# Attention of block 0 first, sixteen plain weight chunks for blocks 0 and 1, and block 1's projection with two tiles in flight

## The chip, the cores and the metric

The kernel runs on one core of one Trainium2 chip. The metric is the device time of one execution in microseconds (us). The engines are PE (TensorE, matrix products into PSUM banks), DVE (VectorE), ACT (ScalarE), POOL (GpSimd) and SP (SyncE, which here only issues transfers). Each engine works through its own queue in order: an instruction that waits holds up all that stand behind it.

## The reference

One pre-LN block in float32, for one sequence of 2048 tokens of width 576, with 32 heads of width 18:

```python
def _A_ref(x, wqkv, wo):
    ...
    W, dil = 8, 2
    idx = pos[:, None] - off[None, :]          # off = arange(W) * dil
    logits = jnp.einsum("bhsd,bhswd->bhsw", q, kg) * scale
    logits = jnp.where(mask[None, None, :, :], logits, -1e9)
    attn = _softmax(logits, axis=-1)
    o = jnp.einsum("bhsw,bhswd->bhsd", attn, vg)
    return (lambda x, *d: x.transpose(*d))(o, 0, 2, 1, 3).reshape(B, S, D) @ wo

def _B_ref(x, w_gate, w_up, w_down):
    g = jnp.einsum("bsd,df->bsf", x, w_gate)
    u = jnp.einsum("bsd,df->bsf", x, w_up)
    h = _sigmoid(g) * u
    return jnp.einsum("bsf,fd->bsd", h, w_down)

h = x + _A_ref(_layernorm(x, axis=-1), A_wqkv, A_wo)
h2 = h + _B_ref(_layernorm(h, axis=-1), B_w_gate, B_w_up, B_w_down)
```

A token sees itself and seven tokens before it, two apart. The hidden width F of the gated part is 4608.

## The kernel before

**Tiling.** Since the window steps by two, even and odd tokens never meet. The tokens fall into four blocks of 512: blocks 0 and 1 are the two halves of the even tokens, blocks 2 and 3 those of the odd ones. A block is four tiles of 128 tokens. Every product in full precision is built of three fast ones: an operand is split into a high part (ACT, L100) and the rest (DVE, L101), by the function `split`; the tiles `th` and `tl` hold split activations, `qw`, `w` and `d` split weights.

**First part.** `ln1` normalises a block (DVE statistics, POOL's power, ACT applying them for blocks 1 to 3: L126 to L128), transposes it on PE and splits it. `qkv` computes q, k and v for one of four groups of eight heads; ACT evicts them (L346) and writes them to DRAM (`q`, `k`, `v`). `attention` reads q and windows of k and v back (`kw`, `vw`) and works on DVE alone but for one exponential on ACT: sixteen steps for one block and group. The result of block 0 stays in SBUF, the others go through `oscr`. `att_all` sets the order (0,0), (1,0), (0,1), (1,1), (0,2), (0,3), (1,2), (1,3), each (block, group); its steps are handed out between the tiles of `qkv`. The loop at the end of this part drains what is left of `att_all` and then runs block 0's output projection, `proj_j`, for four tiles at once: transpose of the attention result, split, two products with halves of `wo` (L146 to L149), residual, a second normalisation, transpose. That gives block 0's operands `a00` and `a01`.

**Second part.** The hidden width is walked in 36 chunks of 128, for two blocks at a time. A *plain* chunk (`single`, "std") handles one block: 28 products of 128x512 (tiles b) for gate and up, and 24 of 128x288 for the down product (tile `dp`). A *pair* chunk (`pair`) handles two blocks with seven products in place of eight, built from sums and differences of the two blocks' operands (`sums`, `s1` to `s4`): 50 of 128x512 and 48 of 128x288. The order of the list `items` is: NSTD plain chunks for block 0, the pair chunks NSTD to 35 for blocks 0 and 1, NSTD plain chunks for block 1, 36 pair chunks for blocks 2 and 3; NSTD is 8, so there are 80. Weights come one chunk ahead: `load_gu` loads the gate and up columns (tile `wg`, 640 KB, two buffers, issued two chunks ahead), `weights` loads the down rows (tile `wd`, 288 KB, one buffer) and splits both. `down_units` sums two chunks in PSUM, ACT copies them to `stage` (L612), and POOL adds them to DRAM with an accumulating transfer (`h<-stage`, L616).

**Background work.** Each chunk calls `bg_step` at seven places; each call takes one step of a generator. `under_first` runs under the plain chunks of block 0: `proj_scr` projects block 1, tile after tile (load of `oj`, `proj_j` in one PSUM bank `bgp`, write of `xj` to `xscr`), then `operands` reads blocks 0 and 1 back (`ar`), forms the sums and splits them. `finish_bg` empties it before the first pair chunk. `under_rest` does the same for blocks 2 and 3 under what follows: attention, projection, operands. A scheduler puts the instructions on each engine in an order of its own, by priorities (`tc.high_priority`) and a model of when operands are ready; the background work moves in this order against the chunks that emit it.

Of the kernel before, what the change touches and what calls it, by code (L numbers as in the profile page):

```python
# [14 lines left out]
F32 = mybir.dt.float32  # L15
# [37 lines left out]
HC = 700  # L53
NSTD = 8


@with_exitstack
def kernel(ctx, tc, x, wqkv, wo, wmlp, out):
# [96 lines left out]
    def attention(at, b, g, o):  # L155
# [66 lines left out]
    def proj_j(bank, oj, hj, wos, th, tl, xn_tile, put, order=(0, 1)):  # L222
        with tc.high_priority(HI):
            dve.tensor_copy(oj[:, D:DX], oj[:, DM:D])
        pv = tr_main(bank(), oj)
        with tc.high_priority(HI):
            split(th[:, 0:4], tl, pv)
        yield
        pv = tr_rest(bank(), oj)
        with tc.high_priority(HI):  # L230
            split_rest(th[:, 4], pv)
        yield
        for i in order:
            ps = bank()
            tok_major(ps, DH2, th, tl, slice(0, P), wos[i][:, 0], wos[i][:, 1])
# [12 lines left out]
        pv = tr_rest(bank(), xn)  # L248
        with tc.high_priority(HI):
            put(pv.unsqueeze(1), slice(4, 5))  # L250
        yield

    def sums(pl, ar, s1, s2, s4, rd):
        a00, a01, a10, a11 = ar[0][:, 0:2], ar[0][:, 2:4], ar[1][:, 0:2], ar[1][:, 2:4]
# [4 lines left out]
        dve.tensor_tensor(rd, ar[0][:, 4], ar[1][:, 4], ALU.subtract)  # L261
        return dict(a00=(a00, None), s2=(s2, None), s3=(a10, None), s1=(s1, None),
                    a01=(a01, ar[0][:, 4]), a11=(a11, ar[1][:, 4]), s4=(s4, rd))

# [90 lines left out]
    o = None  # L355
    emitted = set()

    def att_all():
# [8 lines left out]
    xb = load_x(0)  # L367
    w = qkv_w(0)
    T = []
    gl = ln1(0, xb)  # L370
    T.append(next(gl))
    xb = load_x(1)
    run(gl, qkv(0, 0, T[0], w))
    pads(0)
    for b in (1, 2, 3):
        if b > 1:
            xb = load_x(b)
        gl = ln1(b, xb)
        T.append(next(gl))
        drain(gl)  # L380
        if b == 1:
            drain(qkv(1, 0, T[1], w))
    ag = att_all()
    wn = qkv_w(1)
    for b in (2, 3):
        for _ in qkv(b, 0, T[b], w):
            step(ag, 2)
    pads(1)
    w = wn
    w2 = qkv_w(2)  # L390
    for b in range(4):
        for _ in qkv(b, 1, T[b], w):
            step(ag, 2)
    pads(2)
    pads(3)
    w3 = qkv_w(3)

    def wo_w(i, ww):
# [5 lines left out]
        act.dma_start(wscr[i], f32(ww))  # L404
        return ww

    wos = [None, wo_w(1, sar.tile([P, 2, 5, DH2], F32R, name="wo1"))]
    for b, g in ((0, 2), (1, 2), (0, 3), (1, 3), (2, 2), (3, 2), (2, 3), (3, 3)):
        if (b, g) == (2, 3):
            wos[0] = wo_w(0, saw.tile([P, 2, 5, DH2], F32R, tag="qw", bufs=2, name="wow"))  # L410
        for _ in qkv(b, g, T[b], w2 if g == 2 else w3):
            step(ag, 3)
    h = load_x(0)
    drain(ag)

# [5 lines left out]

    with tc.high_priority(HI):
        ar = tok_tile((P, 5, TB))
        oT = th_tile(), tl_tile()
        xn = [ev_tile([P, 2, DX]) for _ in range(2)]
        gens = []
        for j in range(NS):
            js = slice(j * P, (j + 1) * P)

            def put(pv, cs, js=js):  # L430
                act.activation(ar[:, cs, js], pv, AF.Copy)

            gens.append(proj_j(any_bank, o[:, j], h[:, j], wos, oT[0][:, :, js], oT[1][:, :, js],
                               lambda j=j: xn[j // 2][:, j % 2], put, (1, 0)))
        run(*gens)
        act.dma_start(hacc[0], h)
        act.dma_start(xscr[0], ar)
        X = {"a00": x_half(ar[:, 0:2], None), "a01": x_half(ar[:, 2:4], ar[:, 4])}
    ps_stk.close()
# [10 lines left out]
    def load_gu(f):  # L450
        ws = gw.tile([P, GU], F32, bufs=2, name="wg")
        sp.dma_start(ws, wmlp[f][:, :GU])
        return ws

    def weights(kind, f, ws):
        with tc.high_priority(HI):
            wd = gw.tile([P, D], F32, name="wd")
            sp.dma_start(wd, wmlp[f][:, GU:WC])
            r = ws.rearrange("p (c n) -> p c n", c=10)
            w1 = gw.tile([P, 2, 5, P], F32R, bufs=2, name="w1")  # L460
# [168 lines left out]

    def proj_scr(pj, blocks):  # L630
        wos = []
        for i in range(2):
            ww = pj.tile([P, 2, 5, DH2], F32R, name=f"wow{i}")
            sp.dma_start(f32(ww), wscr[i])
            wos.append(ww)

        def load(b, j):
            oj = pj.tile([P, DX], F32, bufs=2, name="oj")
            sp.dma_start(oj[:, :D], oscr[b][:, j])
            return oj  # L640

        tiles = [(b, j) for b in blocks for j in range(NS)]
        nxt = load(*tiles[0])
        for i, (b, j) in enumerate(tiles):
            e, hf = BLOCKS[b]
            oj = nxt
            hj = pj.tile([P, D], F32, name="hj")
            sp.dma_start(hj, xv[e, hf][:, j])
            if i + 1 < len(tiles):
                nxt = load(*tiles[i + 1])  # L650
            xj = pj.tile([P, 5, P], F32, name="xj")

            def put(pv, cs):
                act.activation(xj[:, cs], pv, AF.Copy)

            th = pj.tile([P, 5, P], F32R, name="oth")
            tl = pj.tile([P, 4, P], F32R, name="otl")
            yield from proj_j(lambda: gp.tile([P, 512], F32, name="bgp"), oj, hj, wos, th, tl,
                              lambda: xj.rearrange("p c n -> p (c n)"), put)
            act.dma_start(hacc[b][:, j], hj)  # L660
            act.dma_start(xscr[b][:, :, j * P:(j + 1) * P], xj)

    def operands(pp, p, Xn, names):
        ar = []
        for t in range(2):
            a = pp.tile([P, 5, TB], F32, name=f"ar{t}")
            sp.dma_start(a, xscr[2 * p + t])
            ar.append(a)
        s = [pp.tile([P, 2, TB], F32, name=f"rs{i}") for i in range(3)]
        rd = pp.tile([P, TB], F32, name="rd")  # L670
        raw = sums(pp, ar, *s, rd)
        yield
        for n in names:
# [5 lines left out]
    def under_first():  # L679
        drain_at()  # L680
        with sb_pool("pj", "right") as pj:
            yield from proj_scr(pj, (1,))
        with sb_pool("pp", "right") as pp:
            yield from operands(pp, 0, X, ("s2", "s3", "s1", "a11", "s4"))

    def drain_at():
        at_stk.close()

    Xn = {}

    def under_rest(last_x):
        with sb_pool("at2", "right") as at2:
# [4 lines left out]
            yield from ga  # L697
        with sb_pool("pj2", "right") as pj:
            yield from proj_scr(pj, (2, 3))
        pp = ctx.enter_context(sb_pool("pp2", "right"))  # L700
# [6 lines left out]
    def bg_step(i):  # L707
        nonlocal raw, phase
        if phase is ATT and i == 3:
            return  # L710
# [35 lines left out]
    wg = load_gu(1)  # L746
    seg = []
    for c, (kind, p, f) in enumerate(items):
        w, d = wc
        if c == NSTD:  # L750
            finish_bg()
            last_x = splits[-1]
            bg = under_rest(getattr(last_x, "ins", last_x))
        if c == NF:
            with tc.high_priority(HI):
                a10 = gw.tile([P, 2, TB], F32, tag="tw", name="tw")
                sp.dma_start(a10, xscr[1][:, 0:2])
                X["a10"] = x_half(a10, None)
        if c == NF + NSTD:
# [12 lines left out]
        else:  # L772
            hid = pair(X, w, units, bg_step)
            blocks = [2 * p, 2 * p + 1]
# [49 lines left out]
```

## Time and profile before

| what | value |
|---|---|
| median of three runs | 1720.25 us (1715.8 to 1725.97) |
| the execution profiled | 1719.7 us, span 1717.7 us |
| PE busy | 1611.8 us (94%) |
| DVE busy | 1145.2 us (67%) |
| ACT busy | 821.4 us (48%) |
| PE clock granted, mean | 0.97 |
| DMA | 256.64 MB, mean 149 GB/s |

The span is the time from the first to the last instruction on the chip's core; the run is some 2 us longer. The page's slices cut the span in 40 equal parts and give each engine's busy share in tenths. The chain of waits goes back from the last instruction: each row is a start, a duration and what ran or was waited for there. The first product of the second part stands at 256.3 us, the products of blocks 2 and 3 run from about 1060 us to the end.

### The profile page before, as it was taken

The page shows a single profiled execution, that of the slowest core. Times are in us where ns is not written, and L with a number is a line of the kernel's source. Part 1 is how long each engine was busy: PE and PEld are TensorE (multiplying, and loading weights), DVE is VectorE, ACT ScalarE, POOL GpSimd, SP SyncE. Part 2 cuts the span into 40 slices and gives each one's busy share as a digit, 9 for nine tenths or more (in the row PEclk, how much of TensorE's full clock was granted, in tenths as well). Part 3 has the DMA queues.
Part 4 walks back from the last instruction along what each step waited for, and adds up shares of the span by engine and source line. Part 5 has one row for each costly group of instructions (what it writes and reads, how often), then busy time and mean ns, then how long its engine had stood idle before and what let it go on. Part 6 is the DMA issues. An engine that isn't in the chain of part 4 may idle for free.

```text
span 1717.7 us, 22333 instructions
## 1 busy us (share of the span) xinstructions
PE 1611.8 (94%) x8688; PEld 1418.8 (83%) x8688; DVE 1145.2 (67%) x1769; ACT 821.4 (48%) x1419; POOL 102.9 (6%) x112
## 2 busy tenths in 40 slices
PE   5999879955999999999889989999999999999999
PEld 4999868754888888888778977888888888888888
DVE  7699889634998999998545454645454454544544
ACT  7322225422565555555335444555555555555551
POOL 2000000000000000000000000000000000000000
PEclk8999989986999999999999999999999999999999
DMA  5555545753367676665756665545645456455462
GB/s 171 201 192 207 200 151 161 232 143 121 101 162 190 155 177 161 167 156 122 224 135 156 167 185 144 139 111 118 139 101 132 111 119 137 102 127 115 115 146 83
DMA packets 86426, 256.64 MB, mean 149 GB/s; under 512 B 7857, under 2 KB 25521, under 8 KB 84529
## 3 DMA queue, kind: packets, MB, share of 16 engines
q0 software_dynamic: 19040, 82.58, 25.9%
q1 hardware_dynamic: 43856, 142.04, 25.2%
q10 hardware_dynamic: 23424, 30.61, 5.1%
q8 instruction: 68, 1.11, 0.3%
q14 instruction: 38, 0.30, 0.1%
HBM read 141.95 MB, written 115.60 MB: 150 GB/s over the span
## 4 chain that ended last, share of the span: by engine, by line
PE 67%; DVE 15%; DMA 11%; issue 3%; ACT 3%; SPq 0%; POOL 0%; ACTq 0%; DVEq 0%; POOLq 0%
PE b L488 32%; PE dp L606 22%; PE b L495 6%; DMA wd<-in_wmlp_dram 5%; PE acc L146 3%; DMA oj<-o 2%; DVE pr L168 2%; DVE lg L171 2%; PE bgp L146 2%; DVE w L101 2%; DMA wg<-in_wmlp_dram 2%; DVE pr L194 1%; DVE s L501 1%; DVE pr L199 1%; PE bgp L135 1%
## 5 line engine op out<-in xcount | busy, mean ns | idle before, releaser
L488 PE MATMUL b<-tl,w 128*128 128x512 f32 x1728 | 440.1, 399 | 24.4 <-ACT tl L100 18.6
L488 PEld LDWEIGHTS b<-tl,w 128*128 128x128 f32 x1728 | 320.9, 191 | 99.2 <-ACT tl L100 19.6
L488 PE MATMUL b<-th,w 128*128 128x512 f32 x1344 | 347.8, 393 | 5.7 <-DVE w L101 3.5
L488 PEld LDWEIGHTS b<-th,w 128*128 128x128 f32 x1344 | 248.4, 189 | 57.4 <-DVE w L101 3.9
L612 ACT ACTIVATE stage<-dp 128x576 f32<-128x576 f32 x272 | 175.0, 646 | 127.2 <-PE dp L606 121.3
L606 PE MATMUL dp<-d,h1h 128*128 128x288 f32 x1152 | 214.5, 297 | 4.2 <-ACT stage L612 2.9
L606 PE MATMUL dp<-d,h0h 128*128 128x288 f32 x1152 | 214.3, 297 | 2.2 <-ACT h0h L100 1.8
L606 PEld LDWEIGHTS dp<-d,h1h 128*128 128x128 f32 x1152 | 179.7, 190 | 11.0 <-ACT stage L612 3.4
L606 PEld LDWEIGHTS dp<-d,h0h 128*128 128x128 f32 x1152 | 179.0, 190 | 9.2 <-ACT h0h L100 2.0
L495 PE MATMUL b<-th,w 128*128 128x512 f32 x576 | 178.4, 390 | 0.0
L146 PE MATMUL acc<-qw,th 128*128 128x432 f32 x512 | 157.8, 370 | 1.1 <-ACT qw L100 1.1
L616 POOL DMA_DIRECT2D h<-stage x68 | 81.4, 1197 | 1151.2 <-ACT stage L612 1115.3
L100 ACT ACTIVATE w<-wg 128x640 fp32r<-128x640 f32 (+2 forms) x176 | 105.5, 605 | 62.9 <-PE b L495 36.9
L101 DVE TENSOR_TENSOR w<-tw,w 128x512 fp32r<-128x512 f32 x128 | 87.9, 686 | 70.0 <-ACT w L100 70.0
L101 DVE TENSOR_TENSOR w<-wg,w 128x640 fp32r<-128x640 f32 (+2 forms) x176 | 115.2, 661 | 26.8 <-ACT w L100 26.6
L569 DVE TENSOR_TENSOR s<-s,b 128x512 f32<-128x512 f32 x64 | 43.8, 685 | 126.6 <-PE b L495 126.5
L495 PEld LDWEIGHTS b<-th,w 128*128 128x128 f32 x576 | 108.3, 188 | 22.7
L606 PE MATMUL dp<-d,h1l 128*128 128x288 f32 x576 | 124.9, 299 | 0.3 <-DVE h1l L101 0.3
L606 PE MATMUL dp<-d,h0l 128*128 128x288 f32 x576 | 124.6, 298 | 0.2 <-DVE h0l L101 0.2
L100 ACT ACTIVATE w<-tw 128x512 fp32r<-128x512 f32 x128 | 80.8, 631 | 89.1 <-PE b L488 81.5
L146 PEld LDWEIGHTS acc<-qw,th 128*128 128x128 f32 x512 | 98.9, 194 | 7.5 <-ACT qw L100 1.4
L146 PE MATMUL acc<-qw,tl 128*128 128x432 f32 x256 | 94.5, 369 | 0.4 <-DVE tl L101 0.4
(188 smaller groups left out, 2115.5 us busy)
## 6 DMA issues: line engine op xcount, KB each, us to landing
h<-stage POOLq DMA_DIRECT2D x68, 1152.0 KB, 9.5
wg<-in_wmlp_dram SPq DMA_DIRECT2D x80, 640.0 KB, 3.9
wd<-in_wmlp_dram SPq DMA_DIRECT2D x80, 288.0 KB, 3.8
kw<-k SPq DMA_DIRECT2D x16, 792.0 KB, 4.5
vw<-v SPq DMA_DIRECT2D x16, 792.0 KB, 5.9
h<-in_x_dram SPq DMA_DIRECT2D x20, 288.0 KB, 4.0
wow<-wo SPq DMA_DIRECT2D x4, 1440.0 KB, 8.2
ar<-x SPq DMA_DIRECT2D x4, 1280.0 KB, 6.4
```

Source lines behind the costliest of these rows:

```text
L100: act.activation(hi, src, AF.Copy)
L101: splits.append(dve.tensor_tensor(lo, src, f32(hi), ALU.subtract))
L135: pe.transpose(ps[:, c * P:(c + 1) * P], xn[:, c * P:(c + 1) * P], ident)
L146: pe.matmul(ps[:, :n], a[:, c, js], m[:, c], start=k == 0, stop=False)
L168: dve.tensor_tensor(pr[:, i], kw[:, j:j + W], q[:, j].unsqueeze(1).broadcast_to([P, W, CG]), ALU.mult)
L171: dve.tensor_reduce(lg[:, 2 * u:2 * u + 2].rearrange("p j w h -> p (j w h)"), pr.rearrange("p j w (h d) -> p (j w h) d", d=DH), AX.X, ALU.add)
L488: pe.matmul(ps, wt[:, a, k0 + c], xx[:, m + c], start=first and k == 0, stop=k == 5, skip_group_check=True)
L495: pe.matmul(ps, wt[:, a, k0], xx[:, 4], start=False, stop=a == 1, skip_group_check=True)
L569: dve.tensor_tensor(s2, s2, b3, ALU.add)
L606: pe.matmul(ps[:, i, :DH2], a[:, js], d[:, m, i * DH2:(i + 1) * DH2], start=k == 0, stop=k == n)
L612: act.activation(hv, ps[:, :, :DH2], AF.Copy)
L616: pool.dma_start(hacc[b], hs, accum_op=ALU.add, max_dma_last_dim=8 * D)
```

## The change

The diff, cut to its core:

```diff
-NSTD = 8
+NSTD = 16
...
-        lg = sm.tile([P, NS, W, HG], F32, name="lg")
+        lg = sm.tile([P, NS, W, HG], F32, bufs=1, name="lg")
...
-    def sums(pl, ar, s1, s2, s4, rd):
+    def sums(a0, a1, s3, s1, s2, s4, rd):
...
-        dve.tensor_tensor(a10, a00, a10, ALU.subtract)
+        dve.tensor_tensor(s3, a00, a10, ALU.subtract)
+        yield
...
-        for b, g in ((0, 0), (1, 0), (0, 1), (1, 1), (0, 2), (0, 3), (1, 2), (1, 3)):
+        for b, g in ((0, 0), (0, 1), (1, 0), (0, 2), (0, 3), (1, 1), (1, 2), (1, 3)):
...
+            if (b, g) == (0, 3):
+                ready.append(b)
...
+    xb = load_x(2)
+    heads(((0, 1), (1, 0)), w, 1)
+    norm(2, xb, 1)
+    xb = load_x(3)
+    heads(((2, 0),), w, 2)
+    norm(3, xb, 1)
+    heads(((3, 0),), w, 2)
...
+    for b, g in ((1, 3), (2, 3), (3, 3)):
+        for _ in qkv(b, g, T[b], w[g]):
+            if ready:
+                next(fr, END)
+                step(ag, 1)
+            else:
+                step(ag, 4)
+    while not ready:
+        step(ag, 1)
+    with tc.high_priority(HI):
+        drain(fr)
...
-        ws = gw.tile([P, GU], F32, bufs=2, name="wg")
-        sp.dma_start(ws, wmlp[f][:, :GU])
+        ws = gw.tile([P, WC], F32, bufs=2, name="wg")
+        sp.dma_start(ws, wmlp[f])
...
-            wd = gw.tile([P, D], F32, name="wd")
-            sp.dma_start(wd, wmlp[f][:, GU:WC])
+            wd = ws[:, GU:WC]
...
+        todo = list(range(NS))
+        live = []
+        n = 0
+        while todo or live:
+            if todo and (not live or (len(live) < 2 and n % 9 >= 4)):
+                live.append(tile_j(todo.pop(0)))
+            for gn in list(live):
+                if next(gn, END) is END:
+                    live.remove(gn)
+                    n = 4
+                else:
+                    n += 1
+                    yield
+        if raw is not None:
+            act.dma_start(xscr[b][:, 0:2], raw[:, 0:2])
...
     def under_first():
-        drain_at()
+        for _ in ag:
+            yield ATT
+        at_stk.close()
+        a1 = xt.tile([P, 5, TB], F32, tag="th", bufs=3, name="ar")
         with sb_pool("pj", "right") as pj:
-            yield from proj_scr(pj, (1,))
+            yield from proj_scr(pj, 1, a1)
...
+        while c < NF:
+            yield ATT
+        for b in (2, 3):
+            with sb_pool(f"pj{b}", "right") as pj:
+                yield from proj_scr(pj, b, None)
...
-        if c == NF:
-            with tc.high_priority(HI):
-                a10 = gw.tile([P, 2, TB], F32, tag="tw", name="tw")
-                sp.dma_start(a10, xscr[1][:, 0:2])
-                X["a10"] = x_half(a10, None)
...
-            hid = pair(X, w, units, bg_step)
+            hid = pair(X, w, units, last_pair if c == NF - 1 else bg_step)
```

- NSTD goes from 8 to 16: sixteen plain chunks for block 0 and sixteen for block 1, and 20 pair chunks for the two; 88 chunks in all.
- Attention takes block 0's four groups within its first five places. Normalisation of blocks 2 and 3 (`norm`) now stands behind the first products of blocks 0 and 1. Block 0's projection is a generator (`front`); its steps stand between the tiles of the last three `qkv` calls. What remains of block 1's attention is stepped under the plain chunks.
- One transfer of 928 KB a chunk brings `wg` and what was `wd`, in two buffers.
- `proj_scr` takes one block, with up to two tiles in flight, into `th` and `tl` tiles of a whole block. It writes the normalised tile into `oj`, keeps one half of `wo` in two `tl` tiles, and has two `hj` and two `xj`. Block 1's transposed result stays in SBUF (`a1`, in a slot of `th`) in place of a write to `xscr` and a read; only its first two fifths are still written there. `last_pair` reads them back in the last pair chunk of blocks 0 and 1 (before: one chunk later).
- `sums` yields after each operation, and the third sum has a tile of its own. Plain chunks leave out the fifth of the seven places. The projection of blocks 2 and 3 waits for the second plain chunks.

The next rows show what stands on the engines at three places. A row is a line, an operation, and output<-input.

First place: ACT, where the first q, k and v of block 0 are evicted (L346 before, L351 after); L127 and L128 belong to a block's normalisation, `th` to its split, `qw` to the weights of a group. Before:

```order
L127 ACTIVATE tok<-tok,rstd 128x576 x2
L128 ACTIVATE tok<-tok 128x64
L100 ACTIVATE th_609<-mm 128x4x128
L128 ACTIVATE tok<-tok 128x64
L100 ACTIVATE th_609<-mm 128x4x128
L100 ACTIVATE qw<-ws 128x432 x3
L346 ACTIVATE ev<-acc 128x3x144 x3
L100 ACTIVATE qw<-ws 128x432 x2
L346 ACTIVATE ev<-acc 128x3x144
```

After:

```order
L100 ACTIVATE th<-mm 128x4x128
L127 ACTIVATE tok<-tok,rstd 128x576
L100 ACTIVATE qw<-ws 128x432
L128 ACTIVATE tok<-tok 128x64
L100 ACTIVATE qw<-ws 128x432 x3
L351 ACTIVATE ev<-acc 128x3x144 x3
L100 ACTIVATE qw<-ws 128x432
L351 ACTIVATE ev<-acc 128x3x144
```

`th_609` is block 3's tile. Ahead of the first eviction ACT had 12 each of L126, L127 and L128 and 16 splits of `th`; now it has 8 each and 11.

Second place: PE, at block 1's projection. Before, it stands in the first pair chunk: from the second product of that chunk on (L488, with the weights `w_3240`), transposes of `oj` (L135, L139) and products with `wo` (L146) are mixed into its first products, and the rows of all four tiles stand ahead of the chunk's products that need block 1:

```order
L606 MATMUL dp<-d,h0h 128x288 x2
L488 MATMUL b_3350<-tl,w_3240 128x512
L135 MATMUL bgp<-ident,oj 128x128 x4
L488 MATMUL b_3350<-tl,w_3240 128x512 x5
L488 MATMUL b_3351<-th,w_3240 128x512 x2
L139 MATMUL bgp<-ident,oj 128x128
L488 MATMUL b_3351<-th,w_3240 128x512 x4
L146 MATMUL bgp<-wow_2411,oth 128x288
```

After, its first tiles stand in the ninth and tenth plain chunk of block 0 (L513 and L520 are their products):

```order
L520 MATMUL b_3004<-th,w_2904 128x512 x2
L135 MATMUL bgp<-ident,oj 128x128 x4
L631 MATMUL dp<-d,h0h 128x288 x2
...
L513 MATMUL b_3005<-tl,w_2908 128x512 x6
L139 MATMUL bgp<-ident,oj 128x128
L513 MATMUL b_3005<-th,w_2907 128x512 x6
...
L135 MATMUL bgp<-ident,oj 128x128 x4
L513 MATMUL b_3135<-tl,w_2989 128x512 x6
L513 MATMUL b_3135<-th,w_2989 128x512
L146 MATMUL bgp<-wow,th 128x288
```

The projection moved from the first pair chunk (number 8) into the plain chunks 8 to 13; the first pair chunk is number 16 and holds none of it.

Third place: ACT, in a plain chunk of block 0 early in the second part: splits of `wg` into `w` (128x640 is needed first, the others follow), splits of the down rows into `d`, the sigmoid (L524 before, L549 after) and the split of the hidden tile (`h0h`). Before:

```order
L524 ACTIVATE s<-b_2399 128x512
L100 ACTIVATE w_2388<-wg 128x256
L100 ACTIVATE w_2518<-wg 128x640
L100 ACTIVATE d<-wd 128x576
L100 ACTIVATE w_2387<-wg 128x384
L100 ACTIVATE h0h<-s 128x512
L524 ACTIVATE s<-b_2533 128x512
```

After:

```order
L549 ACTIVATE s<-b_2318 128x512
L100 ACTIVATE w_2307<-wg 128x256
L100 ACTIVATE w_2371<-wg 128x640
L100 ACTIVATE d<-wg 128x576
L100 ACTIVATE w_2306<-wg 128x384
L100 ACTIVATE h0h<-s 128x512
L549 ACTIVATE s<-b_2386 128x512
```

The rows stand alike; what moved is the source of `d`, from a transfer and a buffer of its own to the last 576 columns of the tile whose other columns the `w` rows split.

More of the change, by code (lines that the diff above doesn't have):

```diff
@@ L638, in load @@
             oj = pj.tile([P, DX], F32, bufs=2, name="oj")
             sp.dma_start(oj[:, :D], oscr[b][:, j])
[L640 to L647, printed above, removed]
+            hj = pj.tile([P, D], F32, bufs=2, name="hj")
             sp.dma_start(hj, xv[e, hf][:, j])
-            if i + 1 < len(tiles):
-                nxt = load(*tiles[i + 1])
-            xj = pj.tile([P, 5, P], F32, name="xj")
+            for _ in range(8 if j == 0 and b < 3 else 2):
+                yield
@@ L653, in put @@
+            xj = None if raw is not None else pj.tile([P, 5, P], F32, bufs=2, name="xj")
             def put(pv, cs):
[L654 to L659, printed above, removed]
-            act.dma_start(hacc[b][:, j], hj)
@@ L661, in proj_scr @@
[L661 to L665, printed above, removed]
+                act.activation(xj[:, cs] if raw is None else raw[:, cs, js], pv, AF.Copy)
+            yield from proj_j(lambda: gp.tile([P, 512], F32, name="bgp"), oj, hj, wos,
+                              th[:, :, js], tl[:, :, js], lambda: oj, put)
+            act.dma_start(hacc[b][:, j], hj)
+            if raw is None:
+                act.dma_start(xscr[b][:, :, js], xj)
@@ L666, in operands, with load @@
+    def operands(pp, p, Xn, names, a1=None):
+        def load(t):
             a = pp.tile([P, 5, TB], F32, name=f"ar{t}")
             sp.dma_start(a, xscr[2 * p + t])
-            ar.append(a)
+            return a
+        a0 = load(0)
+        own = a1 is None
+        if own:
+            a1 = load(1)
         s = [pp.tile([P, 2, TB], F32, name=f"rs{i}") for i in range(3)]
         rd = pp.tile([P, TB], F32, name="rd")
-        raw = sums(pp, ar, *s, rd)
-        yield
+        raw = yield from sums(a0, a1, a1[:, 0:2] if own else a0[:, 0:2], *s, rd)
```

137 lines of the change are left out of this document (77 added, 60 removed).

## The prediction

> **What bounds the kernel now.** I read the page's slices first, then busy time by stage, then the chain of waits where the stages lose time.
>
> ```profile
> span 1717.7 us, 22333 instructions
> ...
> PE   5999879955999999999889989999999999999999
> ...
> DVE  7699889634998999998545454645454454544544
> ```
>
> PE (TensorE) is full in most of the forty slices of 43 us; the holes are at the start and in slices 9 and 10 (both 5), while DVE shows 3 and 4 there, so neither engine is busy. The price of full work comes from a steady stretch of the chain:
>
> ```profile
> 639.31 4.08 PE b L488 x18
> 643.39 0.45 PE b L495 x2
> 643.84 3.18 PE dp L606 x24
> ```
>
> A 128x512 product takes 4.08/18 = 0.2267 us and a 128x288 one 3.18/24 = 0.1325. With these I split the span after the first chunk into five stages. The columns of the views are the window, its length, PE busy with the tile named and its instructions, PE clock, DMA share and GB/s. First tile b (gate and up products), then dp (down products), then bgp (the output projection under the chunks):
>
> ```profile
> 256.30:333.60 77.30, 56.98 (x225) 0.94 0.65 190
> 333.60:454.45 120.85, 39.85 (x150) 0.80 0.45 137
> 454.45:818.65 364.20, 237.46 (x1000) 1.00 0.65 160
> 818.65:1060.30 241.65, 123.03 (x474) 0.96 0.63 168
> 1060.30:1717.70 657.40, 426.64 (x1800) 1.00 0.52 120
> ```
> ```profile
> 256.30:333.60 77.30, 21.72 (x144) 0.94 0.65 190
> 333.60:454.45 120.85, 16.12 (x98) 0.80 0.45 137
> 454.45:818.65 364.20, 134.28 (x962) 1.00 0.65 160
> 818.65:1060.30 241.65, 73.31 (x482) 0.96 0.63 168
> 1060.30:1717.70 657.40, 247.40 (x1778) 1.00 0.52 120
> ```
> ```profile
> 333.60:454.45 120.85, 31.51 (x152) 0.80 0.45 137
> 818.65:1060.30 241.65, 48.66 (x304) 0.96 0.63 168
> ```
>
> A projection tile has 28 products of 128x288 and ten short transposes, 38 instructions; I take 4.5 us for it (28 x 0.1325 = 3.7, and 0.8 for the transposes), so 152 bgp records are four tiles, 18 us, and 304 are eight, 36 us. What each stage loses on PE is its length less b x 0.2267, dp x 0.1325 and the tiles: 77.3 - 51.0 - 19.1 = **7.2**; 120.85 - 34.0 - 13.0 - 18 = **55.8**; 364.2 - 226.7 - 127.5 = **10.0**; 241.65 - 107.5 - 63.9 - 36 = **34.3**; 657.4 - 408.1 - 235.6 = **13.7**. Together 121. The second stage, block 1's projection ahead of the first pair chunk, loses nearly half of it, and runs at a clock of 0.80. Its chain:
>
> ```profile
> 318.55 5.11 DMA o<-kw
> ...
> 324.52 10.93 DMA oj<-o
> ...
> 416.23 3.78 PE b L488 x9
> ```
>
> Block 1's last attention result leaves DVE at 318.55 and is written out; the tile is read back at 324.52; the products that need block 1's operands begin at 416.23. This chain of 97.7 us runs while only a few products are left: the eight plain chunks of block 0 are used up at 333.6.
>
> **The change part by part, from the run profiled (1719.7 us, span 1717.7; the median is 1720.25, so I take them as one).**
>
> *Sixteen plain chunks.* Eight weight chunks go from pair to plain for blocks 0 and 1. A pair chunk has 50 b products, two plain chunks 56; the dp products stay. So 8 x 6 = 48 more products of 0.2267: **+10.9**. In return the plain chunks of block 0 last 16 x (28 x 0.2267 + 24 x 0.1325) = 16 x 9.53 = 152 us, with block 1's four tiles (18) and idle time (19, below) 189, against the 62.2 that pass in before from the first chunk (256.3) to block 1's last attention plus the chain of 97.7: 160. The operands are ready some 29 us before the first pair chunk asks for them, even if two tiles in flight save nothing. PE's new order agrees: the projection's pieces stand in chunks 8 to 13, singly between plain products.
>
> *The 55.8 us go; what is late next?* The new first stage has sixteen plain chunks. Eight lie over the same 1.5 attentions as now and keep the 7.2. The other eight carry four tiles in flight by twos, each step standing in PE's queue, where a late DVE or ACT result stops the products behind it. Their loss lies between 3.6 (half of 7.2) and 17 (half of the fourth stage's 34.3, which carries eight tiles); I take 12, nearer the upper row since it is the same work. So 7.2 + 55.8 becomes 19: **-44**. The pair chunks under attention stay 20 in number (1000/50), and lose 10.0 as now. The fourth stage's successor, blocks 2 and 3 projected under the second sixteen plain chunks, keeps eight tiles and its 34.3: 26 in the chunks and 8 at their end, where the operands of blocks 2 and 3 are emitted in the chunk before they are used. The last 36 pair chunks keep 13.7.
>
> *Attention order, LN and the first chunk.*
>
> ```profile
> 40.00:62.00 22.00, 18.86 (x90) 16.97 (x91) 6.78 (x16) 12.23 (x31) 0.00 (x0) 0.92 0.57 194
> ```
> ```profile
> 39.48 1.44 ACT L126 ACTIVATE tok<-h,nm 128x576 f32<-128x576 f32 x2
> 40.81 1.44 ACT L127 ACTIVATE tok<-tok,rstd 128x576 f32<-128x576 f32 x2
> 42.15 0.25 ACT L128 ACTIVATE tok<-tok 128x64 f32<-128x64 f32 x1
> 42.34 0.60 ACT L100 ACTIVATE th<-mm 128x512 fp32r<-128x512 f32 x1
> ...
> 47.62 0.95 ACT L346 ACTIVATE ev<-acc 128x432 f32<-128x432 f32 x2 [2.68 <-PE acc L149]
> ```
> ```profile
> 62.00 1.36 DVE L168 TENSOR_TENSOR pr<-kw,q 128x1152 f32<-128x1152 f32 x1 [1.15 <-DMA kw<-k]
> ```
>
> Attention begins on DVE at 62.00, after a stretch in which DVE (third busy number) works 6.78 of 22 us: the q and k evictions stand on ACT behind the normalisation of all four blocks. The changed order puts four tiles' LN and five th splits behind these evictions. Two L126 start 1.33 us before the L127 that follows, so one takes 0.67; a tile is 0.67 + 0.67 + 0.19 = 1.5, and the four with five splits of 0.5 are 8.5. DVE, which has the same six and a half attentions and block 0's projection ahead of the first chunk's weights as now, starts earlier by 0 to 8.5; I take 6, because the first eviction (L346) waited 2.68 for PE too. What it fills is idle time, so the first chunk begins at about 250 instead of 256.3: **-6**. The moved splits cost nothing since DVE had that idle time; without it they cost these 6. Front's overlap with the last qkv hides a few PE waits; if it hides none, PE's last product frees the weight buffer no later than now.
>
> *One weight load a chunk.*
>
> ```profile
> wg<-in_wmlp_dram SPq DMA_DIRECT2D x80, 640.0 KB, 3.9
> wd<-in_wmlp_dram SPq DMA_DIRECT2D x80, 288.0 KB, 3.8
> kw<-k SPq DMA_DIRECT2D x16, 792.0 KB, 4.5
> vw<-v SPq DMA_DIRECT2D x16, 792.0 KB, 5.9
> ```
> ```profile
> ACT w L100 <- DMA wg<-in_wmlp_dram: 16.8, 5, 5.0
> ACT d L100 <- DMA wd<-in_wmlp_dram: 13.5, 4, 4.5
> ```
>
> 928 KB in one piece has no row. By 792 KB it lands in 4.5 to 5.9; I take 5.5. The wait rows (total, times, longest) are of 957.7 to 1060.3, the eight plain chunks of block 1: ACT waits 16.8 us for wg and 13.5 for wd. The second goes, since wd has no single buffer any more; the first grows by about 1.6 each time. The next load may be issued only when ACT and DVE have split the last third of the old one. Behind a waiting W1 or d split on ACT stand the sigmoid and the hidden split of the running chunk, for which PE's next bank waits. Cost between -1 and +3 us a plain chunk; I take **0**, as the two rows nearly cancel. The Trainium skill (Perfetto Trace Analysis, section DMA Optimizations) says that splitting a DMA can let work start sooner when the DMA engines are mostly idle, and this change does the opposite; by it the merged load would be the loss priced in the first rival.
>
> *The rest.* Block 1's result kept in SBUF takes out one write and one 1280 KB read in the chain, with nothing on the end while the slack of 29 us holds. Sums one at a time, a third sum tile, one lg buffer and the a10 split one chunk earlier are covered by pair chunks that PE bounds: 0, or up to 5 us in all without that cover.
>
> **Sum:** 1719.7 + 10.9 - 44 - 6 = 1680.6, **1680 us**.
>
> **Rivals.**
> (a) *The merged load ends last; slower.* The first chunk's weights took 8.56 us in the chain:
>
> ```profile
> 245.75 8.56 DMA wg<-in_wmlp_dram
> ```
>
> If 928 KB lands like that in the plain chunks, 3 us after the 5.5 that I allow, and a lead of PE covers 1, each of 32 plain chunks loses 2: +64, 1744. It decides from (1729 - 1680)/32 = 1.5 us a chunk on. For it: the 16.8 above. Against it: the first eight plain chunks lose only 7.2/8 = 0.9 each beside attention. 8%. The Trainium skill (TensorE: Matmul & The Clock Gate, section HAM oscillation — how this bites in real kernels) adds that gaps above some 3.4 us throttle PE again; the clock of 0.80 in the second stage agrees, but no row shows such gaps in every plain chunk.
> (b) *Block 1's chain still ends last*, because its steps now wait behind plain products on PE, DVE and ACT and POOL's queue: 50 us longer, less the slack of 29, is a stall of 21: 1701. With it I count *DVE saturating*: in the 20 attention chunks one more us each gives 1700. 12%.
> (c) *The change doesn't do what it says*: the tiles under the plain chunks stop PE at each of their steps, seven of about 1.4 us by four tiles, 39 us, where I allowed 12, and the first chunk comes no earlier: 1680 + 27 + 6 = 1713. 7%.
> (d) *The gaps close further*: two tiles in flight halve the fourth stage's 34.3 and the first stage's 12: -23, 1657; with a first chunk at 247, 1654. 13%.
>
> **How the numbers follow.** My forecast with its own range of 1660 to 1700 has 60%. The range takes in (d), (b) and the lower part of (c): 1650 to 1713. A measurement of this kernel tells some 0.5% from no change, so faster means under 1711.6, slower over 1728.9: faster 60 + 13 + 12 = 85%, same 7%, slower 8%.
>
> **What would show it.** Right: the first b product near 250; block 1's projection tiles between 325 and 410; the first pair chunk near 440 without a gap above 3 us; slices 9 and 10 at 9; in the second sixteen plain chunks about 26 us idle and a gap under 15 before pair chunks of blocks 2 and 3; 1800 b products in the tail in 657 us. Wrong: ACT waiting for wg in most plain chunks by over 3 us (a); a chain through oj, hj and rstd into the first pair chunk (b); many gaps of 1 to 2 us before bgp (c).

## The result and the profile after

| | median | ratio to before, 95% interval |
|---|---|---|
| before | 1719.1 us (4 runs) | |
| changed | 1673.2 us (4 runs, 1669.9 to 1676.0) | 0.9727 [0.9689, 0.9765] |
| changed, measured again with the last experiments | 1672.3 us (4 runs, 1670.1 to 1675.9) | 0.9734 [0.9712, 0.9756] |

The change saves 2.7%; 1680 had been forecast. The span of the profiled execution falls from 1717.7 to 1673.8 us, by 43.9. The slices of the changed kernel:

```profile
span 1673.8 us, 22256 instructions
...
PE   5999897999999999999799989999999999999999
...
DVE  7699788744999999999444447654544544544544
```

The two fives of PE at slices 9 and 10 have become nines. What is left stands mainly at slice 7 (7), where the first chunk begins, and from slice 20 to 24 (7, 9, 9, 9, 8), where DVE shows 4: the second sixteen plain chunks. By stage, in the same three views as ahead of the prediction (tile b, tile dp, tile bgp):

```profile
263.50:438.50 175.00, 112.20 (x448) 0.98 0.63 185
438.50:788.30 349.80, 235.38 (x1000) 1.00 0.66 172
788.30:1020.80 232.50, 117.06 (x448) 0.94 0.66 190
1020.80:1673.80 653.00, 423.76 (x1800) 1.00 0.52 121
```
```profile
263.50:438.50 175.00, 48.63 (x336) 0.98 0.63 185
438.50:788.30 349.80, 127.58 (x914) 1.00 0.66 172
788.30:1020.80 232.50, 65.63 (x434) 0.94 0.66 190
1020.80:1673.80 653.00, 248.00 (x1777) 1.00 0.52 121
```
```profile
263.50:438.50 175.00, 24.18 (x152) 0.98 0.63 185
438.50:788.30 349.80, 0.00 (x0) 1.00 0.66 172
788.30:1020.80 232.50, 49.83 (x304) 0.94 0.66 190
```

With the same prices (0.2267, 0.1325, 4.5 a tile) PE's loss is 175.0 - 101.6 - 44.5 - 18 = 10.9, 349.8 - 226.7 - 121.1 = 2.0, 232.5 - 101.6 - 57.5 - 36 = 37.4, and 653 - 408.1 - 235.5 = 9.4. The clock of the first plain stage is 0.98, where block 1's projection had 0.80. Beside the forecast:

| term | forecast | measured |
|---|---|---|
| start of the first chunk | 256.3 to 250 (-6) | 256.3 to 263.5 (+7) |
| 48 more products | +11 | +11 |
| loss up to the first pair chunk | 63 to 19 (-44) | 63 to 10.9 (-52) |
| loss of the pair chunks under attention | 10 to 10 | 10.0 to 2.0 (-8) |
| loss of the second plain stage | 34 to 34 | 34.3 to 37.4 (+3) |
| loss of the last 36 pair chunks | 14 to 14 | 13.7 to 9.4 (-4) |
| sum | -39 | -43 |

The last column is read from one profile. The profile of the changed kernel measured again has the first chunk at 261.0, a loss of 34.4 in the second plain stage and the other losses within 0.4 of these, so 3 us in a stage can't be told from noise. Two terms have a surprise in them: the first chunk comes later, not earlier, and the pair chunks under attention, which the change was not thought to touch, lose 8 us less. And the table cannot say which edit does what. That took experiments.

### The profile page after: what moved, and what is told of

It is laid out like the page before. It is cut to its first block, busy times and chain, and to the rows that moved or that the text cites. A ratio compares the mean times of both kernels' runs of the same rounds, so it can differ in the third digit from the quotient of the medians.

```text
span 1673.8 us, 22256 instructions
## 1 busy us (share of the span) xinstructions
PE 1598.2 (95%) x8736; PEld 1418.3 (85%) x8736; DVE 1133.2 (68%) x1745; ACT 818.7 (49%) x1419; POOL 102.1 (6%) x112
## 4 chain that ended last, share of the span: by engine, by line
PE 46%; DMA 3%; DVE 2%; ACT 0%; issue 0%; POOL 0%; SPq 0%; DVEq 0%; POOLq 0%
PE b L513 24%; PE dp L631 16%; PE b L520 4%; DMA wg<-in_wmlp_dram 2%; DMA oj<-o 1%; PE bgp L146 1%; PE bgp L135 0%; DVE w L101 0%; DVE tl L101 0%; DVE th L101 0%; DVE s L526 0%; ACT w L100 0%; PE bgp L139 0%; DVE d L101 0%; PE bgp L148 0%
## 5 line engine op out<-in xcount | busy, mean ns | idle before, releaser
L513 PE MATMUL b<-tl,w 128*128 128x512 f32 x1728 | 433.8, 395 | 10.2 <-ACT w L100 9.8
L513 PEld LDWEIGHTS b<-tl,w 128*128 128x128 f32 x1728 | 319.7, 190 | 73.4 <-ACT w L100 10.2
L513 PE MATMUL b<-th,w 128*128 128x512 f32 x1392 | 361.7, 393 | 0.8 <-ACT s L587 0.7
L513 PEld LDWEIGHTS b<-th,w 128*128 128x128 f32 x1392 | 257.6, 189 | 53.8 <-ACT s L587 1.7
L101 DVE TENSOR_TENSOR w<-wg,w 128x384 fp32r<-128x384 f32 (+2 forms) x208 | 133.2, 645 | 73.8 <-ACT w L100 73.7
L100 ACT ACTIVATE w<-wg 128x384 fp32r<-128x384 f32 (+2 forms) x208 | 122.1, 593 | 121.8 <-PE b L520 50.9
L520 PE MATMUL b<-th,w 128*128 128x512 f32 x576 | 177.9, 390 | 0.4 <-DVE th L105 0.4
L146 PE MATMUL acc<-qw,th 128*128 128x432 f32 x512 | 156.3, 366 | 3.4 <-ACT ev L351 1.7
L101 DVE TENSOR_TENSOR w<-tw,w 128x512 fp32r<-128x512 f32 x112 | 76.8, 687 | 89.2 <-ACT w L100 89.2
L520 PEld LDWEIGHTS b<-th,w 128*128 128x128 f32 x576 | 108.3, 188 | 23.4 <-DVE th L105 0.9
L594 DVE TENSOR_TENSOR s<-s,b 128x512 f32<-128x512 f32 x56 | 38.4, 686 | 122.5 <-PE b L520 122.5
L100 ACT ACTIVATE w<-tw 128x512 fp32r<-128x512 f32 x112 | 70.6, 632 | 89.4 <-PE b L513 84.0
L146 PEld LDWEIGHTS acc<-qw,th 128*128 128x128 f32 x512 | 98.0, 192 | 10.2 <-ACT ev L351 1.9
L168 DVE TENSOR_TENSOR pr<-kw,q 128x1152 f32<-128x1152 f32 x64 | 85.0, 1353 | 18.4 <-DMA kw<-k 17.8
```

The source lines that it names most:

```text
L100: act.activation(hi, src, AF.Copy)
L101: splits.append(dve.tensor_tensor(lo, src, f32(hi), ALU.subtract))
L146: pe.matmul(ps[:, :n], a[:, c, js], m[:, c], start=k == 0, stop=False)
L168: dve.tensor_tensor(pr[:, i], kw[:, j:j + W], q[:, j].unsqueeze(1).broadcast_to([P, W, CG]), ALU.mult)
L513: pe.matmul(ps, wt[:, a, k0 + c], xx[:, m + c], start=first and k == 0, stop=k == 5, skip_group_check=True)
L520: pe.matmul(ps, wt[:, a, k0], xx[:, 4], start=False, stop=a == 1, skip_group_check=True)
```

## The experiments

Ratios are to the kernel before, measured again beside each group of runs; 0.001 is 1.7 us. A wait is shown as who waited and for whom, then its total in us, how often it came, and the longest.

**Sixteen plain chunks alone.**

```diff
 # kernel before
-NSTD = 8
+NSTD = 16
```

> The kernel before with NSTD = 16 and nothing else of the change. Theory (sixteen plain chunks are the cause; they lay cover over block 1's chain of 97.7 us): first chunk at 256, the loss of the first plain stage falls from 7.2 + 55.8 to 25 or less, 48 more products cost 10.9: about 1693 us (1682 to 1700). Rival (the other parts carry it: tiles in flight, block 1's result in SBUF, one weight load): the projection of block 1, still tile after tile, stops PE under the plain chunks nearly as long: 1712 or more.

Measured: 1730.7 us, ratio 1.0071 [1.0051, 1.0092], 0.7% slower than before. The theory fails as it stands, though its stage behaves; the rival has the time but not the reason: the first product comes at 253.8, the first pair chunk at 440.3, and the loss between them is 22 us instead of 63. It is given back at once. The 20 pair chunks under attention (tile b, then tile dp):

```profile
440.30:823.60 383.30, 244.40 (x1000) 0.98 0.61 151
```
```profile
440.30:823.60 383.30, 129.28 (x914) 0.98 0.61 151
```

383.3 - 226.7 - 121.1 = 35.5 us lost, where the kernel before loses 10; and the second plain stage loses 49, where it loses 34. The waits of ACT, DVE and PE in that window (total, times, longest):

```profile
ACT d L100 <- DMA wd<-in_wmlp_dram: 35.2, 10, 6.4
```
```profile
DVE d L101 <- ACT d L100: 14.2, 6, 3.7
DVE w L101 <- ACT w L100: 11.9, 8, 4.6
```
```profile
PE b L488 <- DVE s L563: 11.6, 4, 3.9
PE b L488 <- ACT s L555: 7.5, 5, 4.4
```

Read upwards: PE waits for a sum on DVE, DVE stands before a split whose other half ACT has not made, and ACT stands before the down rows, which have one buffer. The chain of waits shows that loop, and SP's queue shows that the next load could not be issued before DVE had split the last rows (three pieces of the chain, one wait of SP):

```profile
518.85 0.68 DVE d L101
...
519.58 8.28 DMA wd<-in_wmlp_dram
...
527.88 0.69 ACT d L100
```
```profile
SPq L458 <- DVE d L101: 55.5, 16, 10.7
```

Loads of `wd` take 15.7% of the chain between 440 and 825 us. But the waits alone don't give the price: in the kernel before, ACT waits for `wd` under attention too,

```profile
ACT d L100 <- DMA wd<-in_wmlp_dram: 25.7, 7, 5.3
```

and its pair chunks lose 10.0, with 5.0 us of PE's waits seen in place of 23.0.

**All but the sixteen plain chunks.**

```diff
 # changed kernel
-NSTD = 16
+NSTD = 8
```

> The changed kernel with NSTD = 8. Theory (sixteen plain chunks are the cause): block 1's attention and projection end long after the eighth plain chunk, PE waits 40 us or more ahead of the first products that need block 1, and 10.9 us of products go: 1700 to 1725. Rival (two tiles in flight and the result kept in SBUF shorten the chain enough): 1690 or less.

Measured: 1718.2 us, 0.9988 [0.9975, 1.0001], no difference. This is what the theory has: the first pair chunk, with block 1's projection in it, begins at 336.3 and takes until 411.4. The attention of blocks 2 and 3 is no loss any more (3.7 us over 25 pair chunks), but their projection, which waits for the second plain chunks, has eight tiles to put under eight chunks, and from the start of the last of these to the next chunk 75.6 us pass.

So each half of the change is worth nothing or less alone, and together they save 2.7%.

**The second buffer of the down rows.** The merged load does two things: it makes one transfer of two, and it gives the down rows two buffers, since `wg` has two. Three kernels pull these apart. The first keeps two transfers, with two buffers each:

```diff
 # changed kernel
-        ws = gw.tile([P, WC], F32, bufs=2, name="wg")
-        sp.dma_start(ws, wmlp[f])
+        ws = gw.tile([P, GU], F32, bufs=2, name="wg")
+        sp.dma_start(ws, wmlp[f][:, :GU])
+        wd = gw.tile([P, D], F32, bufs=2, name="wd")
+        sp.dma_start(wd, wmlp[f][:, GU:WC])
...
-            wd = ws[:, GU:WC]
...
```

> The changed kernel with the down rows loaded apart again (288 KB, now with two buffers, issued right behind the 640 KB of the gate and up columns). Theory (the merged load costs nothing to speak of, for both pieces are issued together): 1668 to 1678. Rival (the merged load lands too late in the second sixteen plain chunks, where three waits of 8.5 to 9.4 us for wg lie in the chain): their loss of 37 us falls to 25 or less, 1662 or less.

Measured: 1676.5 us, 0.9752 [0.9730, 0.9775]. Its interval overlaps both of the changed kernel: merging as such makes no difference that can be told. The second plain stage loses 34.5 us, not 25, so the waits for wg in its chain are not a matter of one piece or two. (The pair chunks under attention lose 9.4 here; 4.7 of these are one wait of PE for DVE in the first of them, of which more below.) The Trainium skill (Perfetto Trace Analysis, section DMA Optimizations) says that splitting a DMA into smaller pieces may let the task end sooner if the DMA engines are generally idle; here their busy share is 0.63 to 0.67 up to the last 36 pair chunks, and the split gave no gain.

The second kernel goes back to one buffer for the down rows; all else is as in the changed kernel:

```diff
 # changed kernel
-            wd = ws[:, GU:WC]
...
+            wd = gw.tile([P, D], F32, name="wd")
+            sp.dma_start(wd, wmlp[f][:, GU:WC])
...
```

> The changed kernel with the down rows loaded apart into one buffer, as before the change, all else changed. Theory (what the merged load brings is the second buffer of the down rows: with one, ACT waits for wd, as it does for 35 us under attention in the kernel before with sixteen plain chunks, and DVE and PE behind it): the loss of the 20 pair chunks under attention goes from 2 us (9 with two separate buffers) to 20 or more, time 1692 to 1712. Rival (those chunks lose their time for another reason, the order of attention's steps or the tail of block 1's projection): 1682 or less.

Measured: 1712.4 us, 0.9959 [0.9939, 0.9978], 0.4 above the theory's range. Against the changed kernel that is 0.9959 - 0.9727 = 0.023, 40 us, nearly the whole gain. The pair chunks under attention (tile b, then tile dp):

```profile
442.30:815.00 372.70, 241.48 (x1001) 0.99 0.64 164
```
```profile
442.30:815.00 372.70, 127.92 (x914) 0.99 0.64 164
```

372.7 - 226.9 - 121.1 = 24.7 lost instead of 2.0; the first stage loses 17.7 instead of 10.9, the second plain stage 40.5 instead of 37.4, the tail 14.2 instead of 9.4: 37 us in the sum. ACT's wait for wd in the window is 22.7 us (5 times, 5.5 the longest), PE's waits come to 15.8, and SP waits 58.6 us (17 times) for DVE's split of `d` before it can issue `wd`. One thing goes along with the buffer: with one, `wd` is issued one chunk ahead, with two it goes out beside `wg`, two chunks ahead. That SP's queue stands waiting for the buffer speaks for the buffer; no run has two buffers and the later issue.

The third kernel gives the kernel before just two things, the sixteen plain chunks and the second buffer (with the earlier issue):

```diff
 # kernel before
-NSTD = 8
+NSTD = 16
...
     def load_gu(f):
+        wd = gw.tile([P, D], F32, bufs=2, name="wd")
+        sp.dma_start(wd, wmlp[f][:, GU:WC])
...
-            wd = gw.tile([P, D], F32, name="wd")
-            sp.dma_start(wd, wmlp[f][:, GU:WC])
...
     def proj_scr(pj, blocks):
...
+        ww = [tl_tile().rearrange("p c n -> p (c n)")[:, :5 * DH2]
+              .rearrange("p (c n) -> p c n", c=5) for _ in range(2)]
...
```

> The kernel before with sixteen plain chunks and two buffers for the down rows, loaded two chunks ahead behind wg; to make room, one half of wo lies in two tl tiles. Theory (these two things make up most of the gain, neither of them alone): the pair chunks under attention lose 10 us or less instead of 35, time 1690 to 1705. Rival (two tiles in flight and the rest are needed): 1715 or more.

Measured: 1686.1 us, 0.9808 [0.9782, 0.9833], better than the theory's range. Two of the edits give some 34 of the change's 46 us. The pair chunks under attention lose 350.3 - 226.9 - 121.1 = 2.3 us, as in the changed kernel:

```profile
445.10:795.40 350.30, 235.65 (x1001) 1.00 0.65 167
```
```profile
445.10:795.40 350.30, 127.46 (x914) 1.00 0.65 167
```

What stays against it is the first plain stage (26.6 lost, against 10.9) and the second (42.2, against 37.4).

**Tiles in flight, and the way through DRAM.**

```diff
 # changed kernel
-            if todo and (not live or (len(live) < 2 and n % 9 >= 4)):
+            if todo and (not live or (len(live) < 1 and n % 9 >= 4)):
```

> The changed kernel with one tile of the projection in flight instead of two. Theory (the slack covers it; two in flight are not what the change lives on): first pair chunk still without a gap over 3 us, loss of the second sixteen plain chunks 37 plus or minus 8, time 1668 to 1682. Rival (two in flight hide the steps' waits): each of twelve tiles loses 2 us or more, and the operands of blocks 2 and 3 come late: 1695 or more.

```diff
 # changed kernel
-        a1 = xt.tile([P, 5, TB], F32, tag="th", bufs=3, name="ar")
...
-            yield from proj_scr(pj, 1, a1)
+            yield from proj_scr(pj, 1, None)
...
-            yield from operands(pp, 0, X, ("s2", "s3", "s1", "a11", "s4"), a1)
+            yield from operands(pp, 0, X, ("s2", "s3", "s1", "a11", "s4"))
```

> The changed kernel with block 1's transposed result written to DRAM tile by tile and read back, as before the change. Theory (slack before the first pair chunk, some 15 us by the trace): no difference, 1669 to 1678. Rival (the chain ends just in time): the first products with block 1's operands wait 5 to 10 us: 1679 to 1684.

Measured: one tile in flight 1683.3 us, 0.9783 [0.9765, 0.9800]; through DRAM 1680.6 us, 0.9766 [0.9734, 0.9799]. They cost some 10 and 7 us, the second not clear of noise by its interval. With one tile the time lies 1.3 above the theory's range, though its signs hold: the second plain stage loses no more than with two (37.1), and no gap in the first pair chunk is above 3 us (PE's longest wait there is 2.1). Through DRAM it is the rival that has both the time and the place. Both edits meet at the first pair chunk: it takes 17.75 us in the changed kernel, 21.8 with one tile and 25.3 through DRAM, where PE waits for a product on DVE that stands among the splits of the late operands:

```profile
442.28 2.93 PE L513 MATMUL b<-th,w 128*128 128x512 f32 x6 [4.23 <-DVE s L526]
```

So the chain of block 1 ends just in time. In the changed kernel its last attention operation, its first split for a pair chunk, its last, and the first products that need one (three rows of DVE, one of PE):

```profile
322.72 0.46 DVE L202 TENSOR_TENSOR kw<-pr 128x288 f32<-128x288 f32 x1
```
```profile
426.68 1.22 DVE L101 TENSOR_TENSOR tl<-rs,tl 128x1024 fp32r<-128x1024 f32 x1
...
437.83 1.22 DVE L101 TENSOR_TENSOR th<-rs,th 128x1024 fp32r<-128x1024 f32 x1
```
```profile
441.70 4.24 PE L513 MATMUL b<-tl,w 128*128 128x512 f32 x18
```

From 323.2, the end of attention, to 427.9, the end of the first split, the chain takes 104.7 us, and 13.8 are left to the first product; but the last split ends only at 439.05, after the chunk has begun.

**The first chunk.** The changed kernel computes q, k and v of (1,2) before those of (0,3), though attention now takes (0,3) fifth:

```diff
 # changed kernel
-    heads(((1, 2), (0, 3), (2, 2), (3, 2)), w, 2)
+    heads(((0, 3), (1, 2), (2, 2), (3, 2)), w, 2)
```

> The changed kernel with the products of (0,3) ahead of those of (1,2), one line. Theory (the first chunk is late, 263.5, because DVE waits 8.8 us for kw of attention (0,3), and block 0's projection, the last qkv and the weight load follow it): that wait goes, the first chunk comes at 254 to 257, time 1663 to 1668. Rival (the first chunk is set by the load of the first weights behind kw of (1,3), which waits for the write of (1,1)'s result, or DVE waits for another attention instead): first chunk at 260 or later, time 1670 or more.

Measured: 1665.0 us, 0.9684 [0.9661, 0.9707]: 8 us better than the changed kernel, as the theory has it. (The interval lies below that of the changed kernel measured again and overlaps the first one by its edge; the slowest of the five runs, 1667.3, is faster than each of the eight of the changed kernel.) DVE's start of attention (0,3) and PE's first product, in the changed kernel:

```profile
178.06 2.63 DVE L168 TENSOR_TENSOR pr<-kw,q 128x1152 f32<-128x1152 f32 x2 [8.78 <-DMA kw<-k]
```
```profile
263.50 2.93 PE L513 MATMUL b<-tl,w 128*128 128x512 f32 x6 [9.84 <-ACT w L100]
```

and with the two swapped:

```profile
167.26 2.63 DVE L168 TENSOR_TENSOR pr<-kw,q 128x1152 f32<-128x1152 f32 x2 [0.34 <-DMA kw<-k]
```
```profile
253.81 2.51 PE L513 MATMUL b<-tl,w 128*128 128x512 f32 x5 [9.30 <-ACT w L100]
```

The wait for k falls from 8.78 to 0.34, and the first product moves up by 9.7, or by 7 against the changed kernel measured again (all variants of the changed kernel with the old order have it between 260.5 and 263.5, the three with the new one between 253.1 and 253.8).

**The second plain stage.** Its longest wait is for an attention tile of the projection, in the chain of the changed kernel:

```profile
820.29 17.88 DMA oj<-o
```

288 KB, issued within 2.3 us behind 1440 KB of `wow`, another `oj`, an `hj` and 928 KB of weights. So the first tile was put ahead of wo:

```diff
 # changed kernel, proj_scr: the loads of wo moved into load_wo()
-        live = []
-        n = 0
+        live = [tile_j(todo.pop(0))]
+        n = 1
+        next(live[0])
+        load_wo()
+        yield
```

> The changed kernel with the first attention tile of a projection (oj, hj) loaded ahead of the halves of wo instead of behind them. Theory (of the 37 us that the second sixteen plain chunks lose, 10 are PE's wait for the first oj, whose 288 KB take 17.9 us beside 1440 KB of wow): that wait falls under 3 us, time 1662 to 1667. Rival (the same bytes land in the same time, and PE waits for wow or wg instead): 1670 or more.

> Both one-place edits together: (0,3) ahead of (1,2), and oj ahead of wo. Theory: they lie in different stages and add up, 1652 to 1660. Rival: one of them gives nothing by itself, and the sum is that of the other.

and then the second tile's loads too, with both edits in:

```diff
+        early = [load_j(j) for j in range(2)]
...
+            oj, hj = early[j] if j < 2 else load_j(j)
```

> The kernel with both one-place edits (products of (0,3) first, first oj ahead of wo), and the second tile's oj and hj ahead of wo too. Theory (PE's wait for oj in the second plain chunks only moved on from the first tile to the second): that wait of 8 to 10 us goes, 1650 to 1657. Rival (it moves on to wow or wg): 1660 to 1667.

Measured: first tile early 1668.9 us, 0.9701 [0.9674, 0.9727]; with the swap 1662.9 us, 0.9677 [0.9653, 0.9700]; second tile early as well 1668.1 us, 0.9709 [0.9688, 0.9730]. PE's waits for oj in the second plain stage (total, times, longest), in the changed kernel and with the first tile early:

```profile
PE bgp L135 <- DMA oj<-o: 12.1, 2, 10.0
```
```profile
PE bgp L135 <- DMA oj<-o: 13.0, 2, 9.7
```

The wait is as long as before and the stage loses 36.5 instead of 37.4: the edit missed its aim. The tile that PE waits for is the second, not the first: in the changed kernel the chain above has the load issued at 820.29, and the first tile's had gone out at 818.42; with the first tile early its load goes out at 806.12 and DVE works on it at 811.18, yet PE's first transposes of the stage stand until 832.12, for a load. So the scheduler has put the second tile's transposes ahead of the first's, and that tile's load was left behind wow. The 4 us in the median can't be told from noise (the intervals overlap), nor the 2 us that both edits have over the swap alone, as the rival of the two together has it. With both tiles early PE's longest waits in the stage are

```profile
PE bgp L139 <- DVE tl L101: 8.2, 1, 8.2
...
PE bgp L135 <- DMA oj<-o: 3.1, 1, 3.1
```

and the chain has a new row:

```profile
813.69 16.04 DMA wg<-in_wmlp_dram
```

The wait for oj goes; the weights, now the ones behind wow, take 16.0 us, ACT stands before them, and the split that PE needs stands behind ACT. The stage loses 34.5, as the changed kernel does when measured again (34.4), and the time is no better: the rival had it, though the time is 1 us above its range. Perhaps wow's 1440 KB should come at another time; that was not tried. The fastest kernel of the study is the changed one with the swap and the first tile early, 3.2% faster than before, of which only the swap's part is shown.

The changed kernel beside the last four:

> The changed kernel itself again, beside the others on one chip, as a measure for the small differences: 1668 to 1678.

Measured: 1672.3 us, as at first; its first product comes at 261.0.

## Why the prediction was right, and where its steps were not

**What bounds the kernel** was read rightly: the hole ahead of the first pair chunk was the thing to win. It gave 52 us, and the other terms of the table together take 9 back. That the sum came so near is partly luck: the term of the first chunk was 13 us too good, and those of the first plain stage, of the pair chunks under attention and of the tail were 8, 8 and 4 us too bad.

**Sixteen plain chunks** ("7.2 + 55.8 becomes 19"): the mechanism is right, 10.9 was measured. But the step gives the whole gain to the cover, and the cover alone makes the kernel slower. The step that failed is the one on the weights: "Cost between -1 and +3 us a plain chunk; I take 0, as the two rows nearly cancel". It weighed ACT's waits for wd against those for wg in block 1's plain chunks alone, and never asked what the one buffer of the down rows does elsewhere once the order is a different one. The second buffer, with the earlier issue that it allows, is worth 40 us in the changed kernel, 23 of them in the pair chunks under attention. The forecast came out right because it carried the losses of those stages over from a kernel in which the single buffer cost little, and the change took that buffer away.

**The first chunk** ("starts earlier by 0 to 8.5; I take 6"): attention began at 56.36 on DVE, 5.6 earlier, as forecast. The error is in what it takes for granted next, that the rest of DVE's work follows without a new gap: attention (0,3) had been moved to the fifth place and its k had not. The first product came at 263.5 in place of 250, a term wrong by 13, of which the swap takes 7 to 10 away; the 4 that are left (253.8 with the swap) were not traced. The order that would have told it, the products of (1,2) ahead of those of (0,3), was in the code.

**The slack of 29 us** was 13.8. By the forecast attention was to end 62.2 after the first chunk, at 312, and the operands to be ready at 410; it ended at 323.2, for the late first chunk, and the chain took 104.7 instead of 97.7, so they came at 427.9, 18 later. The plain stage ended as forecast (438.5, against 250 + 189). So "even if two tiles in flight save nothing" was wrong by some 10 us, and "nothing on the end" by some 7, the latter not clear of noise: those edits are what makes the chain end in time.

**The rest.** The second plain stage (34 forecast, 37.4 and 34.4 measured) and the 48 products (11) were right. The tail's 4 us less are not explained by a run made for it; the kernels with one buffer for the down rows lose 11.9 to 14.2 there, those with two buffers and sixteen plain chunks 8.1 to 9.8, which points to the same cause.

**The rivals.** (a), the merged load ending last: ACT did wait for wg, 24.1 us in the second plain stage (11 times), but two separate loads change nothing that can be told. (b) came close: 13.8 us lay between it and a stall. (c) did not happen: the first plain stage lost 10.9. (d) happened in the first stage and not in the other.

**Still open:** why the same single buffer costs 10 us or less under attention in the kernel before, and 25 to 35 with sixteen plain chunks. DVE's busy time there is the same (343 us in the kernel before, 341 in the one with sixteen plain chunks), and ACT waits for wd about as long (25.7 us, against 35.2 and 22.7); the order of loads on SP's queue is not the same, and no run told these apart. Nor was the second buffer tried with eight plain chunks alone, or without the earlier issue. And the 12 us that sixteen chunks and the buffer leave are not put down to single edits: one tile in flight and the way through DRAM cost 10 and 7, but at the same place, and the new order of the first part was not tried by itself.

## What to carry to other kernels

An edit that looks like tidying, one transfer for two, can carry much of the gain because of the buffer it adds; price the number of buffers apart from the size of the transfer, and in every stage, not only where its waits show now. When a consumer is moved up in an order, move up whoever makes its data in the same edit, and look for that wait in the order before trusting the start of the next stage. Cover and chain are a pair: measure each half of a change alone, since one that buys time and one that uses it can each be worth nothing.

## What the runs showed of the hardware that was not expected

A transfer of 288 KB that in the kernel before lands in a median of 5.0 us took 17.9 us when 2.9 MB had been issued ahead of it on the same queue within 2.3 us, and with the small loads moved ahead the delay met the next one (16.0 us for 928 KB right behind 1440 KB, against a median of 5.5 in the changed kernel). And one buffer for 288 KB of weights a chunk, issued one chunk ahead, with no wait of ACT for it above 5.5 us under attention, cost 2.3% of the kernel against two issued two ahead.
